# The last 64 features of FFN1, stacked into the seven block products

## The chip, the cores and the metric

The kernel runs on one core of a Trainium2 chip. The time is device microseconds from the start to the end of one execution, taken as the median of several runs; the kernel before takes 1108.99 us (three runs, 1108.16 to 1109.24).

A core has a matrix engine (TensorE, PE in the profile, with its weight loads as PEld), a vector engine (VectorE, DVE), an engine for activation functions (ScalarE, ACT), a general engine (GpSimd, POOL) and an engine that here only issues transfers (SyncE, SP). Each executes its instructions in order and waits on semaphores for the others. Transfers between the device's memory and the on-chip memory are put on a queue by SP, ACT or POOL and carried out by 16 DMA engines.

## The reference

A transformer block in which attention and the feed-forward part work on the same normalised input, and both are added to the input. S is 2048 rows, D is 576 features, F is 4608 hidden features; everything is float32.

```python
xn = layernorm(x)                      # over the 576 features, no weights
q, k, v = xn @ wqkv                    # 32 heads of 18 features
# row s attends to rows s, s-2, ..., s-14 (8 keys, window dilated by 2)
attn = softmax(q . k * 18**-0.5)       # over those 8 keys
a = (attn @ v) @ wo
h = xn @ w1 + b1                       # FFN1: 576 -> 4608
h = maximum(h, 0) ** 2                 # squared relu
out = x + a + (h @ w2 + b2)            # FFN2: 4608 -> 576
```

## The kernel before

**Precision.** A float32 number is split into a high part, as TensorE's float32r keeps it (a copy by ScalarE), and a low part, the rest (a subtraction by VectorE). A product is then three matmuls: high by high, low by high, high by low. "Split" below always means this pair of instructions, `..._hi` on ScalarE and `..._lo` on VectorE.

**Tiling.** The 2048 rows are four blocks of 512 (`TB`), b = 0 to 3. Matmuls are 128 by 128 weights against 512 rows. The 576 features are 512 in four chunks of 128, and 64 that are left over (`x4`). For those 64 the operand holds the features twice, once high and once low in the other 64 partitions, so that two matmuls (`left`) do the three products.

**Stages.** Query, key and value for the first blocks; FFN1 for blocks 0 and 1 together, stage s = 0 (`phase_a(0)`); FFN2 and output for block 1, with the queries, keys and values of blocks 2 and 3 (`phase_b0`); FFN1 for blocks 2 and 3, stage s = 1 (`phase_a(1)`); FFN2 and output for block 3 (`phase_b1`). During a `phase_a` the even block's FFN2 runs along, one pair behind.

**A pair.** `ffn_pair(s, p, work)` computes 2 x 128 hidden features for two blocks of rows, p = 0 to 17. The 512 features in two halves, the two hidden tiles and the two row blocks make a 2 by 2 block product, done with seven block products instead of eight: `B11`, `T1`, `T2`, `T3`, `B21`, `B22`, `T4`, where `T` stands for sums of weight blocks. Their other operands are X, and sums of the rows in `SS[1]`, `SS[2]`, `SS[3]`. Each product is six matmuls (two chunks, three split parts). They accumulate in three PSUM banks, `ba`, `bb`, `bc`:

- `B11` into `ba`, copied to `bb` by ScalarE; `T1` into `bc`;
- `T2` onto `bb`; ScalarE copies `bb` to `u[:, 0]`; then `T3` onto `bb`, copied to `u[:, 1]`;
- VectorE adds `bc` and `u[:, 1]`; `B21` onto `ba`; then `B22` onto `bc`, to which VectorE adds `u[:, 0]`; `T4` onto `bb`.

Then relu with bias, and squares, on ScalarE. The left 64 features add four calls of `left`, two matmuls each. Between the products stand four pieces of `work(i)`, seven matmuls each: FFN2 of the pair before. A pair is 42 + 8 + 28 = 78 matmuls.

**Order of the work.** It is written out by hand: in the five engine queues the instructions stand in the order in which the Python code issues them. A pair does besides: the square split of the pair before (`square_lo`), the next pair's FFN1 weights, which in stage 1 come back ready split from device memory (`w1_again`, 1024 KB twice, on ACT's queue), and two w2 splits (`w2_hi`, `w2_lo`, after which SP loads the w2 tile three ahead, `load_w2`).

**Attention** fills VectorE's time. `side(k)` issues k more steps of it. One unit (one row block, eight heads) has 18 steps: eight for query by key (a product and a sum for each of four row groups), one with the maximum and the subtraction, one that begins with the exponential on ScalarE, and eight for the weighted values. A call with `exp=False` stops ahead of the exponential. In stage 1 a pair has `side(3)` after `T1`, `side(2)` after `B22`, and `side(2, False)` at its end; pair 1 has `side(1)` for the first. Queries, keys and values of a unit come through three `kv` buffers, loaded on POOL's queue; `release()` tells that a buffer is free and issues the next load. Output rows of block 1's attention stand in one of the three until `o_hi(1, 4)`.

Other buffers that matter: `w1r` (two), free in stage 1 until the residual of block 2 is loaded into one ahead of pair 17; `mb`, `x40`, `x41`, `x4d` (one each), and `S1`, which holds `SS[1]`.

Of the kernel before, what the change touches and what calls it, by code (L numbers as in the profile page):

```python
# [8 lines left out]
F32 = mybir.dt.float32  # L9
# [7 lines left out]
P = 128  # L17
S, D, F = 2048, 576, 4608
H, DH, W, DIL = 32, 18, 8, 2
TB = 512  # L20
# [22 lines left out]


@with_exitstack
def block_kernel(ctx: ExitStack, tc: tile.TileContext, x, xt, wqkv, wo, w1, b1, w2, b2, out):
# [44 lines left out]
    oscr = {(b, k): dram.tile([P, NJ * G, z - a], F32, name=f"o{b}{k}") for b in range(NB) for k, (a, z) in enumerate(OPART)}  # L91
    mrscr = {b: dram.tile([2 * NJ, P], F32, name=f"mr{b}") for b in range(1, NB)}
    w1scr = [[dram.tile([P, 16 * P], F32, name=f"w1{p}{k}") for k in range(2)] for p in range(NP)]
    hscr = [[dram.tile([P, 2 * TB], F32, name=f"h{s}{p}") for p in range(NP)] for s in range(2)]

    def flat(t, off, parts, n):
# [6 lines left out]
    def tt(out, a, b, op):  # L103
        return nc.vector.tensor_tensor(out=out, in0=a, in1=b, op=op)  # L104
# [80 lines left out]
    def soon(f):  # L185
        if defer[0]:
            later.append(f)
        else:
            f()
# [5 lines left out]
    def normalize(b):  # L195
        open_x(b)
        for a in (0, 2):
            v = xm[b][:, a:a + 2]
            for k, op in enumerate((ALU.subtract, ALU.mult)):
                tt(v, v, mb[b][:, k:k + 1].to_broadcast([P, 2, TB]), op)  # L200
                if k:
                    soon(lambda v=v, a=a: nc.scalar.activation(X[b][:, 0, a:a + 2], v, AF.Copy))
                yield
        for k, op in enumerate((ALU.subtract, ALU.mult)):
            tt(xf[b], xf[b], mb[b][:, k], op)
        soon(lambda: left_hi(x4[b], xf[b]))
# [150 lines left out]
    def release():  # L357
        free[0] += 1
        fetch()
# [174 lines left out]
    def tile_products(b, n, h):  # L534
        hi, lo = products(h[:, 0, n % 2], h[:, 1, n % 2], w2s.pop((b, n)))
        return hi + lo

    hs, prev = {}, {}
    F_BANKS = [(5, 6, 7), (2, 3, 4)]

    def ffn_pair(s, p, work, first=False):
        b0, b1 = 2 * s, 2 * s + 1
        n = s * NP + p
        ba, bb, bc = (bank(i) for i in F_BANKS[s])
        f0, f1 = 2 * p, 2 * p + 1
        last = p == NP - 1
        A11 = lambda k, c: X[b0][:, k, c]
        A12 = lambda k, c: X[b0][:, k, 2 + c]
        A22 = lambda k, c: X[b1][:, k, 2 + c]
        S4 = lambda k, c: X[b1][:, k, c]  # L550
        ss = lambda i: lambda k, c: SS[i][:, k, c]

        def weight(slot, k, c):
            return w1s[n, slot // 4][:, k, slot % 4, c * P:(c + 1) * P]

        def product(to, slot, a, start=False):
            mm = [(weight(slot, 0, c), a(0, c)) for c in range(2)]
            for c in range(2):
                mm += [(weight(slot, 1, c), a(0, c)), (weight(slot, 0, c), a(1, c))]
            for i, (l, r) in enumerate(mm):  # L560
                nc.tensor.matmul(to, l, r, start=start and i == 0, stop=i == len(mm) - 1, skip_group_check=True)  # L561

        def left(to, f, v):
            for k in range(2):
                nc.tensor.matmul(to, weight(LEFT, k, f), v, start=False, stop=k == 1, skip_group_check=True)  # L565

        def relu(to, a, f):
            nc.scalar.activation(to, a, AF.Relu, bias=b1t[:, f:f + 1])  # L568

        def square_hi(r):  # L570
            h = mt.tile([P, 2, 2, TB], F32R, name="h", bufs=3)
            nc.scalar.activation(h[:, 0], r, AF.Square)
            return h

        def square(r):
            nc.scalar.activation(r, r, AF.Square)  # L576
# [12 lines left out]
        before = prev.pop("finish", None)  # L589
        product(ba, B11, A11, start=True)  # L590
        if first:
            nc.tensor.matmul(bb, weight(B11, 0, 0), A11(0, 0), start=True, stop=True, skip_group_check=True)
        nc.scalar.activation(bb, ba, AF.Copy)
        product(bc, T1, ss(1), start=True)
        if before:
            next(before, None)
        if not last:
            w1_again(n + 1, 0) if s else combine_w1(n + 1)
        if not first:
            side(1 if p == 1 else 3 if s else 2 + p % 2, s == 1)  # L600
# [6 lines left out]
        nc.scalar.activation(u[:, 0], bb, AF.Copy)  # L607
        if not first:
            left(bc, 1, x4[b1])
        work(1)  # L610
        if before:
            next(before, None)

        def splits():
            if not own_w2:
                w2_lo()
            if not last and not s:
                w1_hi(n + 1, 0)
            if not own_w2:
                w2_hi()  # L620
            if not last and not s:
                w1_lo(n + 1, 0)
            if not own_w2:
                w2_lo()

        if not first:
            splits()
        product(bb, T3, ss(3))
        if first:
            left(bc, 1, x4[b1])  # L630
        nc.scalar.activation(u[:, 1], bb, AF.Copy)
# [12 lines left out]
        relu(r0[:, 0], ba, f0)  # L644
        work(2)

        def third():
            product(bc, B22, S4)
            left(bc, 1, x4["d"])
            if not first:  # L650
                side(2)
            tt(r0[:, 1], bc, u[:, 0], ALU.add)
            relu(r0[:, 1], r0[:, 1], f1)

        def fourth():
            product(bb, T4, A22)
            left(bb, 0, x4[b1])
            relu(r1[:, 0], bb, f0)

        if first:  # L660
            fourth()
            third()
            work(2.5)
            h0 = square_hi(r0)
            square(r0)
        else:
            third()
            h0 = square_hi(r0)
            square(r0)
            fourth()  # L670
        side(2, False)
        hs[n] = h0
        prev["r"] = r0, r1, h0
        prev["finish"] = finish_pair()
        work(3)

    def phase_a(s, filler):
# [3 lines left out]
        for p in range(1, NP):  # L681
            h, ops = hs.pop(s * NP + p - 1), []

            def work(i):
                if i in (0, 2):
                    ops.extend(tile_products(b, 2 * p - 2 + i // 2, h))
                add(b, ops[7 * i:7 * i + 7])

            if p == NP - 1:
                complete(b)  # L690
                regroup(b, 0)
                regroup(b, 1)
                residual(b)
                if s == 0:
                    load_xt(2)
                    load_mb(2)
            ffn_pair(s, p, work)
        h, end = hs.pop(s * NP + NP - 1), prev.pop("finish")
        load_h(s, 0)
        next(end)  # L700
# [53 lines left out]
    def o_hi(b, c):  # L754
# [17 lines left out]
        nc.vector.transpose(t[:, 0].rearrange("p (u k f) -> p u k f", k=2, f=n),  # L772
                            ob[b, 1][:, :, None, OB - n:].to_broadcast([P, NJ * G, 2, n]))
        if b == 1:
            release()
        nc.scalar.activation(t[:, 1].bitcast(F32R), t[:, 0], AF.Copy)

    def o_lo(b, c):
# [16 lines left out]
    def residual(b):  # L795
        if b == 1:
            xr[b] = [mt.tile([P, NC - 1, TB], F32, name="h", bufs=3)]
        else:
            xr[b] = [sb.tile([P, NC - 1, TB], F32, name="w1r", bufs=2)]
        nc.sync.dma_start(xr[b][0], xt[b, :, :NC - 1])  # L800
# [179 lines left out]
    def phase_b0():  # L980
# [120 lines left out]
        def filler(i):  # L1101
            if i < 2:
                quads(1, 1, [len(steps) - 2 + i])
            if i == 1:
                for g in (2, 3):
                    offer(2, g)
                for g in range(G):
                    offer(3, g)
# [401 lines left out]
```

## Time and profile before

| | us |
|---|---|
| median of three runs | 1108.99 |
| the profiled execution | 1108.98 |
| its span, first to last instruction | 1107.3 |
| TensorE busy in the span | 1099.9 |
| VectorE busy | 871.6 |
| ScalarE busy | 558.7 |
| GpSimd busy | 115.8 |

The granted TensorE clock is 0.999 over the span. The mean of all transfers is 255 GB/s.

In the stage that is edited, from 652.5 to 951.5 us of the span (pairs 1 to 17 with s = 1), VectorE is busy for 219.0 of 299.0 us, ScalarE for 148.8.

How to read it: the page gives busy time by engine, the chain of work that ended last, and the costliest groups of instructions by line of the code. A row of a timeline has the start and the length in us, the engine, the line, the operation, the tiles written and read, and in square brackets how long the engine stood idle before and what ended that. `L104` is the helper for every VectorE operation on two tensors, so such rows are told apart by their tiles. Windows give the busy time of each engine in a stretch of the span. A DMA's "landing" is the time from its issue to its completion.

### The profile page before, as it was taken

The page shows a single profiled execution, that of the slowest core. Times are in us where ns is not written, and L with a number is a line of the kernel's source. Part 1 is how long each engine was busy: PE and PEld are TensorE (multiplying, and loading weights), DVE is VectorE, ACT ScalarE, POOL GpSimd, SP SyncE. Part 2 cuts the span into 40 slices and gives each one's busy share as a digit, 9 for nine tenths or more (in the row PEclk, how much of TensorE's full clock was granted, in tenths as well). Part 3 has the DMA queues.
Part 4 walks back from the last instruction along what each step waited for, and adds up shares of the span by engine and source line. Part 5 has one row for each costly group of instructions (what it writes and reads, how often), then busy time and mean ns, then how long its engine had stood idle before and what let it go on. Part 6 is the DMA issues. An engine that isn't in the chain of part 4 may idle for free.

```text
span 1107.3 us, 13777 instructions
## 1 busy us (share of the span) xinstructions
PE 1099.9 (99%) x4966; PEld 928.2 (84%) x4966; DVE 871.6 (79%) x1148; ACT 558.7 (50%) x787; POOL 115.8 (10%) x219
## 2 busy tenths in 40 slices
PE   9999999999999999999999999999999999999998
PEld 7998888888888888888899888888888888888887
DVE  7686979897996979999979477686767778699655
ACT  5435765556566654455344345454554545533342
POOL 4000101020020100100010200210202102010100
PEclk9999999999999999999999999999999999999999
DMA  8956987889799686866755976858668596665862
GB/s 297 333 179 237 336 297 257 301 199 361 261 246 379 232 351 213 310 232 227 255 169 160 324 267 238 318 187 308 230 244 292 194 332 241 229 219 199 279 189 85
DMA packets 97332, 282.56 MB, mean 255 GB/s; under 512 B 12904, under 2 KB 41328, under 8 KB 82544
## 3 DMA queue, kind: packets, MB, share of 16 engines
q1 hardware_dynamic: 62336, 182.90, 47.7%
q0 software_dynamic: 10544, 52.14, 13.2%
q10 hardware_dynamic: 24384, 46.64, 12.9%
q8 instruction: 39, 0.64, 0.2%
q14 instruction: 29, 0.24, 0.1%
HBM read 200.16 MB, written 81.48 MB: 254 GB/s over the span
## 4 chain that ended last, share of the span: by engine, by line
PE 95%; DVE 2%; DMA 1%; issue 1%; ACT 0%; POOL 0%; ACTq 0%; DVEq 0%; POOLq 0%
PE p L530 45%; PE p L561 30%; PE p L332 7%; PE p L565 6%; PE p L937 6%; PE p L941 1%; PE p L1294 1%; DMA w1s<-w 1%; DVE pr L104 0%; DVE w2s L104 0%; PE p L1211 0%; DVE h L104 0%; DVE w1s L104 0%; PE p L1256 0%; DVE r L104 0%
## 5 line engine op out<-in xcount | busy, mean ns | idle before, releaser
L530 PE MATMUL p<-h,w2s 128*128 128x512 f32 x2066 | 491.7, 389 | 0.3 <-DVE w2s L104 0.2
L530 PEld LDWEIGHTS p<-h,w2s 128*128 128x128 f32 x2066 | 387.6, 188 | 81.9 <-DVE w2s L104 0.6
L561 PE MATMUL p<-X,w1s 128*128 128x512 f32 x864 | 219.3, 389 | 0.0
L561 PEld LDWEIGHTS p<-X,w1s 128*128 128x128 f32 x864 | 162.2, 188 | 33.6
L503 ACT ACTIVATE w2s<-w2r 128x640 fp32r<-128x640 f32 x164 | 120.1, 735 | 138.2 <-PE p L530 112.8
L104 DVE TENSOR_TENSOR w2s<-w2r,w2s 128x576 fp32r<-128x576 f32 x164 | 123.4, 754 | 70.8 <-ACT w2s L503 70.6
L561 PE MATMUL p<-S,w1s 128*128 128x512 f32 x648 | 164.7, 389 | 0.5 <-ACT r L607 0.5
L561 PEld LDWEIGHTS p<-S,w1s 128*128 128x128 f32 x648 | 121.5, 188 | 26.1 <-ACT r L607 0.9
L409 POOL DMA_DIRECT2D o<-q x128 | 69.4, 607 | 593.5 <-DVE q L104 591.6
L568 ACT ACTIVATE r<-r,b1t 128x512 f32<-128x512 f32 x72 | 52.0, 722 | 130.5 <-DVE r L104 130.5
L381 DVE TENSOR_REDUCE lg<-pr 128x64 f32<-128x1152 f32 x64 | 86.5, 1352 | 1.5
L104 DVE TENSOR_TENSOR pr<-lg,kv 128x1152 f32<-128x1152 f32 x64 | 86.7, 1355 | 1.2
L104 DVE TENSOR_TENSOR pr<-q,kv 128x1152 f32<-128x1152 f32 x64 | 86.6, 1353 | 0.8
L104 DVE TENSOR_TENSOR r<-p,r 128x512 f32<-128x512 f32 (+1 forms) x77 | 53.0, 689 | 35.3 <-PE p L565 22.7
L104 DVE TENSOR_TENSOR pr<-pr 128x576 f32<-128x576 f32 (+1 forms) x128 | 77.6, 606 | 3.2
L576 ACT ACTIVATE r<-r 128x1024 f32<-128x1024 f32 x72 | 76.2, 1058 | 1.2
L104 DVE TENSOR_TENSOR h<-r,h 128x1024 fp32r<-128x1024 f32 (+3 forms) x46 | 51.8, 1137 | 29.4 <-ACT r L576 20.7
L565 PE MATMUL p<-x,w1s 128*128 128x512 f32 x216 | 66.6, 390 | 0.2 <-DMA w1s<-w 0.2
L104 DVE TENSOR_TENSOR w1s<-w1r,w1s 128x1024 fp32r<-128x1024 f32 (+1 forms) x42 | 50.3, 1199 | 16.7 <-ACT w1s L471 13.7
L607 ACT ACTIVATE r<-p 128x512 f32<-128x512 f32 x36 | 21.6, 600 | 68.1 <-PE p L561 67.7
L568 ACT ACTIVATE r<-p,b1t 128x512 f32<-128x512 f32 x72 | 48.4, 673 | 0.9 <-DMA out<-r 0.5
L565 PEld LDWEIGHTS p<-x,w1s 128*128 128x128 f32 x216 | 40.5, 188 | 9.0 <-DMA w1s<-w 0.6
(172 smaller groups left out, 1092.7 us busy)
## 6 DMA issues: line engine op xcount, KB each, us to landing
w2r<-in_w SPq DMA_DIRECT2D x144, 320.0 KB, 3.6
kv<-kvq POOLq DMA_DIRECT2D x29, 1296.0 KB, 8.4
w<-w1s SPq DMA_DIRECT2D x36, 1024.0 KB, 8.5
w1s<-w ACTq DMA_DIRECT2D x34, 1024.0 KB, 5.9
h<-r SPq DMA_DIRECT2D x36, 512.0 KB, 6.4
h<-h SPq DMA_DIRECT2D x36, 512.0 KB, 3.9
w1r<-in_w SPq DMA_DIRECT2D x18, 640.0 KB, 7.5
kvq<-st ACTq DMA_DIRECT2D x48, 216.0 KB, 3.2
```

The source lines that it names most:

```text
L104: return nc.vector.tensor_tensor(out=out, in0=a, in1=b, op=op)
L332: nc.tensor.matmul(p[:, :QW], l, r, start=k == 0, stop=k == len(mm) - 1)
L381: nc.vector.tensor_reduce(out=lg[:, j * HG:(j + 1) * HG].rearrange("p a w -> p w a"), in_=pr.rearrange("p w (a d) -> p w a d", d=DH), axis ...
L409: nc.gpsimd.dma_start(rows[:, i], q[i * L:(i + 1) * L, :, a:z])
L503: nc.scalar.activation(w2s[stream[i]][:, :DE], raw2[i], AF.Copy)
L530: nc.tensor.matmul(yp[b][c], v, a, start=c not in yb[b], stop=c in last and c not in [o[0] for o in ops[i + 1:]], skip_group_check=True)
L561: nc.tensor.matmul(to, l, r, start=start and i == 0, stop=i == len(mm) - 1, skip_group_check=True)
L565: nc.tensor.matmul(to, weight(LEFT, k, f), v, start=False, stop=k == 1, skip_group_check=True)
L568: nc.scalar.activation(to, a, AF.Relu, bias=b1t[:, f:f + 1])
L576: nc.scalar.activation(r, r, AF.Square)
L607: nc.scalar.activation(u[:, 0], bb, AF.Copy)
L937: nc.tensor.matmul(to, l[:, js], r, start=start and n == 0, stop=n == len(mm) - 1, skip_group_check=True)
```

## The change

In pairs 2 to 17 of stage 1 the left 64 features are treated as two halves of 32, as the 512 are as two halves of 256, and so take part in the same seven block products. For each of the seven there is a stack of 128 partitions: the 32 features' high part, their low part, their high part again, and 32 partitions of zeros; the weights stand against it as high, high, low, low. One matmul does the three split products. So `left` returns at once in these pairs, and each product gets a seventh matmul, at its end:

```diff
+            if stacked:
+                mm.append((LW[p % 2][:, STACK[slot]], ST[slot]))
...
         def left(to, f, v):
+            if stacked:
+                return
```

A pair then has 49 + 28 = 77 matmuls.

*The row stacks.* After the normalisation of blocks 2 and 3, SP stores their 64 left features in device memory (`xlscr`). In pair 0, a memset clears the last 32 partitions of a `w1r` tile, and six loads on SP bring the 32-feature halves back three times over (`load_left_rows`). In pair 1 VectorE makes the four sums (`stack_sums`) in the `kv` buffer that block 1's attention output leaves at `o_hi(1, 4)`; it is released only in pair 2, after the last stack is made. Splits turn rows and sums into the seven stacks: four in the other `w1r` buffer (pair 1), one in `x40` (pair 1), two in `x41` and `x4d` (pair 2).

```diff
+        if ready:
+            left_weight_sums()
+        if s and p == 2:
+            one_stack(T3, "x41")
+            one_stack(B22, "x4d")
+            one_stack_lo(T3)
+            one_stack_lo(B22)
+            release()
+        if s and p == 1:
+            stack_sums()
+            open_stacks()
+            stack_hi(LR["st"][:, 0:2], LR["a"][:, 0:2])
+            stack_hi(ST[T4], LR["a"][:, 3])
         if not first:
             side(1 if p == 1 else 3 if s else 2 + p % 2, s == 1)
...
+            if ready:
+                left_weight_hi(p + 1)
+            if s and p == 1:
+                stack_lo(LR["st"][:, 0:2], LR["a"][:, 0:2])
+                stack_lo(ST[T4], LR["a"][:, 3])
+                stack_hi(ST[T1], LR["s"][:, 0])
             if not own_w2:
                 w2_hi()
...
+            if ready:
+                left_weight_lo(p + 1)
             if not own_w2:
                 w2_lo()
...
+        if s and p == 1:
+            open_left_weights()
+            load_left_weights(2)
+            stack_lo(ST[T1], LR["s"][:, 0])
+            one_stack(T2, "x40")
         work(2)
...
             product(bc, B22, S4)
             left(bc, 1, x4["d"])
-            if not first:
+            if s and p == 1:
+                one_stack_lo(T2)
+                left_weight_sums()
+                left_weight_hi(2)
+            elif not first:
                 side(2)
...
+        if s and p == 1:
+            left_weight_lo(2)
         side(2, False)
```

*The weight stacks.* A new input `w1l` holds the left weights of each pair, repeated to 128 partitions (256 KB a pair). For the pair that follows, SP loads them into the `mb` buffer, VectorE makes the sums, ScalarE and VectorE split them into one of two halves of a `w1r` buffer; the load for the pair after goes out behind the split:

```diff
+    def left_weight_sums():
+        r = LR["w"]
+        tt(r[:, 0:2], r[:, 3:5], r[:, 2:4], ALU.subtract)
+        tt(r[:, 3], r[:, 4], r[:, 0], ALU.subtract)
+        tt(r[:, 6], r[:, 5], r[:, 3], ALU.subtract)
+
+    def left_weight_hi(p):
+        nc.scalar.activation(LW[p % 2], LR["w"], AF.Copy)
+
+    def left_weight_lo(p):
+        rows = slice(2 * L, P)
+        tt(LW[p % 2][rows], LR["w"][rows], LW[p % 2][rows].bitcast(F32), ALU.subtract)
+        load_left_weights(p + 1)
```

In pairs 2 to 16 these are the three parts marked `ready`; for pair 2 they are done in pair 1.

*What moves.* Pair 1 has no `side(2)` after `B22`. The `release()` at `o_hi(1, 4)` moves to pair 2. The residual of block 2 is loaded after pair 17 into `S1`, no longer ahead of pair 17 into a `w1r` buffer.

More of the change, by code (lines that the diff above doesn't have):

```diff
@@ L45, in block_kernel @@
 @with_exitstack
-def block_kernel(ctx: ExitStack, tc: tile.TileContext, x, xt, wqkv, wo, w1, b1, w2, b2, out):
+def block_kernel(ctx: ExitStack, tc: tile.TileContext, x, xt, wqkv, wo, w1, b1, w2, b2, w1l, out):
     nc = tc.nc
@@ L93, in block_kernel @@
     w1scr = [[dram.tile([P, 16 * P], F32, name=f"w1{p}{k}") for k in range(2)] for p in range(NP)]
+    xlscr = {b: dram.tile([2 * L, TB], F32, name=f"xl{b}") for b in (2, 3)}
     hscr = [[dram.tile([P, 2 * TB], F32, name=f"h{s}{p}") for p in range(NP)] for s in range(2)]
@@ L205, in normalize @@
             tt(xf[b], xf[b], mb[b][:, k], op)
+        if b in xlscr:
+            nc.sync.dma_start(xlscr[b], xf[b][:2 * L])
         soon(lambda: left_hi(x4[b], xf[b]))
@@ L536, in tile_products, with load_left_rows, stack_sums, stack_hi @@
         return hi + lo
+    ST, LW, LR = {}, {}, {}
+    STACK = {T1: 0, T3: 1, B11: 2, T2: 3, B22: 4, B21: 5, T4: 6}
+    def load_left_rows():
+        t = LR["a"] = sb.tile([P, 4, TB], F32, name="w1r", bufs=2)
+        nc.vector.memset(t[3 * L:], 0.0)
+        for g in range(3):
+            for k, b in enumerate((2, 3)):
+                nc.sync.dma_start(t[g * L:(g + 1) * L, 2 * k:2 * k + 2], xlscr[b].rearrange("(q r) t -> r q t", q=2))
+    def stack_sums():
+        a, z = LR["a"], LR["s"]
+        tt(z[:, 0], a[:, 2], a[:, 3], ALU.add)
+        tt(z[:, 2], a[:, 0], a[:, 2], ALU.subtract)
+        tt(z[:, 1], z[:, 0], a[:, 0], ALU.subtract)
+        tt(z[:, 3], a[:, 1], z[:, 1], ALU.subtract)
+    def stack_hi(to, v):
+        nc.scalar.activation(to, v, AF.Copy)
+    def stack_lo(to, v):
+        rows = slice(L, 2 * L)
+        tt(to[rows], v[rows], to[rows].bitcast(F32), ALU.subtract)
+    def open_stacks():
+        t = LR["st"] = sb.tile([P, 4, TB], F32R, name="w1r", bufs=2)
+        for i, k in enumerate((B11, B21, T4, T1)):
+            ST[k] = t[:, i]
+    def one_stack(k, name):
+        ST[k] = mt.tile([P, TB], F32R, name=name)
+        stack_hi(ST[k], LR["s"][:, {T2: 1, T3: 2, B22: 3}[k]])
+    def one_stack_lo(k):
+        stack_lo(ST[k], LR["s"][:, {T2: 1, T3: 2, B22: 3}[k]])
+    def open_left_weights():
+        t = sb.tile([P, 2, 7, P], F32R, name="w1r", bufs=2)
+        LR["w"] = sb.tile([P, 7, P], F32, name="mb")
+        LW[0], LW[1] = t[:, 0], t[:, 1]
+    def load_left_weights(p):
+        if p < NP:
+            nc.sync.dma_start(LR["w"][:, 2:6], w1l[p])
+    def left_weight_sums():
[9 more added lines that the diff above has]
+        load_left_weights(p + 1)
     hs, prev = {}, {}
@@ L546, in ffn_pair @@
         last = p == NP - 1
+        stacked = s == 1 and p > 1
+        ready = s == 1 and p > 1 and not last
         A11 = lambda k, c: X[b0][:, k, c]
@@ L692, in phase_a @@
                 regroup(b, 1)
-                residual(b)
                 if s == 0:
+                    residual(b)
                     load_xt(2)
@@ L697, in phase_a @@
             ffn_pair(s, p, work)
+        if s:
+            residual(b)
         h, end = hs.pop(s * NP + NP - 1), prev.pop("finish")
@@ L774, in o_hi @@
         if b == 1:
-            release()
+            LR["s"] = sb.tile([P, 4, TB], F32, name="kv", bufs=3)
         nc.scalar.activation(t[:, 1].bitcast(F32R), t[:, 0], AF.Copy)
@@ L797, in residual @@
             xr[b] = [mt.tile([P, NC - 1, TB], F32, name="h", bufs=3)]
+        elif b == 2:
+            xr[b] = [mt.tile([P, NC - 1, TB], F32, name="S1")]
         else:
@@ L1104, in filler @@
             if i == 1:
+                load_left_rows()
                 for g in (2, 3):
@@ L1487 @@
     w1 = np.concatenate(w1, 2).reshape(NP, P, 5, 2 * P)
+    w1l = np.asarray(B_w1)[DM:].reshape(2, L, NP, 2, P)
+    w1l = np.stack([w1l[q, :, :, f] for q, f in ((0, 0), (0, 1), (1, 1), (1, 0))], 2)
+    w1l = np.tile(w1l.transpose(1, 0, 2, 3), (1, G, 1, 1))
     x = np.asarray(A_x).reshape(S, D)
@@ L1498 @@
         "b2": rows(np.asarray(B_b2).reshape(D, 1)).reshape(NC, P).T,
+        "w1l": w1l,
     }
```

## The prediction

> **What bounds the kernel now.** I read the first and fourth parts of the page, then the busy time by stage, then the chain of waits inside the stage that is edited.
>
> ```profile
> span 1107.3 us, 13777 instructions
> PE 1099.9 (99%) x4966; PEld 928.2 (84%) x4966; DVE 871.6 (79%) x1148; ACT 558.7 (50%) x787; POOL 115.8 (10%) x219
> PE 95%; DVE 2%; DMA 1%; issue 1%; ACT 0%; POOL 0%; ACTq 0%; DVEq 0%; POOLq 0%
> ```
>
> TensorE is busy for 99% of the span and makes 95% of the chain that ends last: a matmul less is time less, as long as nothing makes TensorE wait. The stages (columns: stretch, length, busy time of PE, PEld, DVE, ACT, POOL, granted clock, DMA share, GB/s):
>
> ```profile
> 652.50:951.50 299.00, 299.00 (x1321) 247.56 (x1320) 218.98 (x271) 148.83 (x207) 37.54 (x69) 1.00 0.74 264
> 652.50:670.20 17.70, 17.70 (x80) 14.64 (x79) 11.89 (x17) 7.15 (x10) 0.54 (x1) 1.00 0.95 349
> 670.20:687.90 17.70, 17.70 (x80) 14.66 (x79) 13.49 (x20) 9.17 (x14) 0.00 (x0) 1.00 0.59 211
> ```
>
> The first row is pairs 1 to 17 of the second FFN1 stage, the next two are pair 1 and pair 2. TensorE has no idle time there, the clock is 1.00, and VectorE is busy for 219 of 299 us. The chain over pair 2 (start, length, what):
>
> ```profile
> 670.21 2.72 PE p L561 x12
> 672.93 1.59 PE p L530 x7
> ...
> 686.30 1.59 PE p L530 x7
> ```
>
> It is TensorE alone. By the code a pair holds 78 matmuls (42 in products, 8 left, 28 of FFN2), and from 670.21 to 686.30 + 1.59 = 687.89 they take 17.68 us: 0.2267 us for one.
>
> **The gain.** Pairs 2 to 17 lose 8 left matmuls each and get 7 stacked ones of the same 128x512 shape: 16 x 0.2267 = **3.63 us**. The stacked weights fill all 128 rows, the left ones did too; nothing in the trace prices rows. [...]
>
> **Steady pairs (3 to 17).** Every pair up to 16 gets, for the next pair, on VectorE three weight sums (128x256, 128x128, 128x128) and one low part (64x896), on ScalarE one high part (128x896), on SP one 256 KB load. Prices (line, columns: total, mean ns):
>
> ```profile
> L104 DVE TENSOR_TENSOR w2s<-w2r,w2s 128x576 fp32r<-128x576 f32 x36 | 27.1, 754 | 31.6 <-ACT w2s L503 31.6
> L104 DVE TENSOR_TENSOR h<-r,h 128x1024 fp32r<-128x1024 f32 x16 | 19.6, 1226 | 7.8 <-ACT r L576 7.1
> L104 DVE TENSOR_TENSOR q<-pr 128x144 f32<-128x144 f32 x24 | 7.4, 308 | 0.8
> L104 DVE TENSOR_TENSOR lg<-lg,mx 128x256 f32<-128x256 f32 x7 | 3.0, 425 | 0.2
> L104 DVE TENSOR_TENSOR h<-p,h 128x512 f32<-128x512 f32 x4 | 2.5, 684 | 0.0
> L381 DVE TENSOR_REDUCE lg<-pr 128x64 f32<-128x1152 f32 x26 | 35.1, 1351 | 0.5
> ```
> ```profile
> L576 ACT ACTIVATE r<-r 128x1024 f32<-128x1024 f32 x32 | 33.8, 1058 | 0.5
> L503 ACT ACTIVATE w2s<-w2r 128x640 fp32r<-128x640 f32 x34 | 25.0, 734 | 24.5 <-PE p L530 24.5
> ```
>
> Sums: 0.43 + 0.31 + 0.31 = 1.05 us; the low part lies between 0.75 (576) and 1.23 (1024), by length 1.09; the high part between 0.73 and 1.06, 0.95. Pair 7 has the softmax's exponential at its start, the worst place, so I lay them in there:
>
> ```profile
> 758.45 1.52 PE L561 MATMUL p<-X,w1s 128*128 128x512 f32 x6
> ...
> 758.91 1.23 DVE L104 TENSOR_TENSOR h<-r,h 128x1024 fp32r<-128x1024 f32 x1 [0.33 <-ACT r L576]
> ...
> 764.31 0.60 ACT L607 ACTIVATE r<-p 128x512 f32<-128x512 f32 x1 [1.77 <-PE p L561]
> ...
> 766.35 0.74 ACT L503 ACTIVATE w2s<-w2r 128x640 fp32r<-128x640 f32 x1 [1.44 <-PE p L530]
> ...
> 767.13 0.76 DVE L104 TENSOR_TENSOR w2s<-w2r,w2s 128x576 fp32r<-128x576 f32 x1 [1.85 <-ACT w2s L503]
> ...
> 768.35 0.69 DVE L104 TENSOR_TENSOR r<-p,r 128x512 f32<-128x512 f32 x1 [0.46 <-ACT r L631]
> ...
> 770.91 1.52 PE L561 MATMUL p<-X,w1s 128*128 128x512 f32 x6
> ```
>
> The sums delay the exponential, and by it the copy of the T2 product (764.31), by 1.05; that copy idles 1.77 now. The high part goes into the 1.44 before the second w2 split. VectorE takes 1.05 + 1.09 = 2.14 into the idle 1.85 + 0.46 = 2.31. The addition at 768.35 must be over when B22 (770.91) overwrites its bank; it is 1.9 us early, which covers what is left over. So I cost these at nothing. Without that cover each of 15 pairs would pay up to 2.1 us. The load is issued after the low part, which follows the copy and the high part: 764.31 + 0.60 + 0.95 + 1.09 = 767.0 at the earliest and with T2 ending later some 767.7, 9.2 us into the pair. It is read behind the square split, 758.91 + 1.23 - 758.45 = 1.7 us into the next. A pair being 77 x 0.2267 = 17.46, the load has 9.9 us. The slowest w2 load of pairs 2 to 17 is in pair 9:
>
> ```profile
> DMA to landing us min/median/max: 9.8/10.3/10.7
> ```
>
> So a late one costs VectorE 0 to 0.8 us, inside the 1.9 us; I take 0.
>
> **The way in: pairs 1 and 2.** Here the stacks are built, and the cover is thin. Pair 1 gets on VectorE four 128x512 sums, low parts of 1024, 512, 512 and 512 columns, the weight sums and the low part; it loses the two side steps of its third slot. What stands there now:
>
> ```profile
> 656.24 0.74 DVE L104 TENSOR_TENSOR w2s<-w2r,w2s 128x576 fp32r<-128x576 f32 x1
> 656.91 1.34 DVE L381 TENSOR_REDUCE lg<-pr 128x64 f32<-128x1152 f32 x1
> ...
> 661.05 0.76 DVE L104 TENSOR_TENSOR w2s<-w2r,w2s 128x576 fp32r<-128x576 f32 x1 [2.13 <-ACT w2s L503]
> ...
> 670.05 1.52 PE L561 MATMUL p<-X,w1s 128*128 128x512 f32 x6
> ...
> 673.11 0.40 ACT L390 ACTIVATE lg<-lg 128x256 f32<-128x256 f32 x1
> 673.41 0.73 ACT L503 ACTIVATE w2s<-w2r 128x640 fp32r<-128x640 f32 x1
> ```
>
> Consecutive VectorE rows overlap by 0.07 (656.24 + 0.74 against 656.91), which I take off each. Until the second w2 low part is done: 656.24 + 0.74 + 4 x 0.68 + 1.34 + 0.75 + 1.23 + 0.68 + 0.75 - 7 x 0.07 = 664.0. SP issues the w2 load behind it, then the first stacked-weight load, at about **664.3**. Call its landing L. From L, in the order of the code: sums 1.05, high part 0.95, low part 1.09: the weights are ready at L + 3.1. TensorE wants them at pair 2's seventh matmul, 670.05 + 6 x 0.2267 = **671.4**. Behind the waiting sums on VectorE stands the addition that frees B22's bank for pair 2's T1 (due one matmul after 671.4): at L + 1.05 + 0.69 it is earlier than the weights, and adds nothing. VectorE goes on: two side steps 2.70, pair 1's square split 1.23, sums 1.05, two stack low parts 1.37, then the softmax maximum and subtraction (0.84; the lost steps move them here: before, pair 1 did them and pair 2 began with the exponential), then on ScalarE exponential 0.40, w2 split 0.73, copy of T2 0.60. Sum 8.9, less 8 x 0.07, and so L + **11.5**. T3 overwrites that bank 35 matmuls into pair 2, at 670.05 + 7.93 = **678.0**; each product being one longer gives no more than that. Any L over 666.5 stalls TensorE, us for us.
>
> How soon does the load land? The nearest rows are the 320 KB w2 loads on the same queue (minimum, median, maximum), over the stage, in pair 1 and in quiet pair 5:
>
> ```profile
> DMA to landing us min/median/max: 2.8/6.1/11.6
> ```
> ```profile
> DMA to landing us min/median/max: 2.8/9.7/11.6
> ```
> ```profile
> DMA to landing us min/median/max: 2.8/2.8/2.8
> ```
>
> Pair 1 is the crowded one (DMA share 0.95), but one of its transfers goes away, this attention load on POOL:
>
> ```profile
> 664.52 0.54 POOL L354 DMA_DIRECT2D kv<-kvq  x1 [16.79 <-DVE pr L104]
> ```
>
> POOL's k load for the next head group now waits for a side step after L, and its v load for the buffer that the stack sums keep until pair 2; both are read a pair later, and only the outputs of that attention queue behind them. So I take the stage's median, 6.1: L = 664.3 + 6.1 = 670.4. Then the stacked weights are 673.5 - 671.4 = 2.1 us late, and T3's bank 670.4 + 11.5 - 678.0 = **3.9 us** late, the first included in the second. The second weight load is issued at L + 3.1 and wanted at L + 6.8; I cost it at nothing because the SP queue is then empty, with 2.8 us as in the quiet pair. Bounds of this part: 0 (L below 666.5) to 664.3 + 11.6 + 11.5 - 678.0 = 9.4 us.
>
> **The rest.** In pair 0 a memset of 2048 columns is at most two of the 128x1024 rows, 2.45 us:
>
> ```profile
> 632.34 0.69 DVE L104 TENSOR_TENSOR r<-p,r 128x512 f32<-128x512 f32 x1 [1.69 <-PE p L565]
> 632.95 1.29 DVE L767 STREAM_TRANSPOSE r<-kv 128x512 f32<-128x512 f32 x2
> 635.37 1.29 DVE L104 TENSOR_TENSOR h<-r,h 128x512 fp32r<-128x512 f32 x2 [1.12 <-ACT h L768]
> ```
>
> It takes 1.69 idle us and pushes the next rows by 0.8, inside the 1.12 idle ahead of 635.37. The six row loads on SP and the two row stores of the stage before are read tens of us later; they hold SP behind a VectorE result that the following w2 load waits past anyway. The residual moves behind pair 17, ahead of an h load on SP; both are read only after FFN2's last two tiles and part of the o chunks. All at nothing; if the cover were gone, a 1024 KB transfer ahead of the h load.
>
> **Sum.** Profiled time 1108.98 (the median of the runs is 1108.99): 1108.98 - 3.63 + 3.9 = **1109.3 us**. The gain of sixteen pairs is paid back on the way into the second of them.
>
> **Rivals.**
> - *The first load lands as in a quiet queue* (2.8 us; for it: its rival on POOL is gone; against it: w1s and two w2 loads are still moving). L = 667.1, no wait for weights, T3 0.6 late: 1108.98 - 3.63 + 0.6 = **1106.0**. Faster by 0.2% needs L under 667.9, a landing under 3.6 us. [...]
> - *The first load lands as pair 1's w2 loads do* (9.7 to 11.6). T3 7.5 to 9.4 late: **1112.9 to 1114.8**. This is the other side; it decides from a landing of 8.0 us on, where the stall is 5.8.
> - *The second load is the late one*: 6.1 us instead of 3.7 makes VectorE wait 2.4 more ahead of the exponential: **1111.7**. For it: pair 2's w1s load starts close behind it.
>
> **How the numbers follow.** About 0.2% (2.2 us) is what a measurement of this kernel can tell. Forecast, within 0.2%: 0.48. Quiet load: 0.22, faster. Slower: crowded first load 0.15, late second load 0.15, together 0.30. The likeliest has 1106.8 to 1111.2 for its own; the range goes down to the quiet case less 0.2 and up to the low end of the crowded one, 1105.8 to 1112.9.
>
> **What would show it.** Right: 77 matmuls in 17.46 us in pairs 3 to 17 without idle TensorE; in pair 2 a wait of TensorE for VectorE at the first stacked matmul and one for ScalarE's T2 copy, together 3.9 us; the weight sums of pair 1 waiting for the load. Wrong: no wait in pair 2 (a quiet load, or steps in another order), waits at B22 in many pairs, or a stall at the stage's ends.

## The result and the profile after

The changed kernel takes 1115.24 us, median of six runs (1113.80 to 1115.48), against 1108.93 for the kernel before: a ratio of 1.0054, 95% interval 1.0041 to 1.0067. It is slower, and above the predicted range. The profiled execution has 6.5 us more span. The first part of the page:

```profile
span 1113.8 us, 13890 instructions
PE 1102.4 (99%) x4950; PEld 926.3 (83%) x4950; DVE 912.0 (82%) x1223; ACT 575.5 (52%) x809; POOL 115.2 (10%) x219
```

TensorE has 16 matmuls fewer (4950 for 4966), as foretold, and is busy for 2.5 us longer. Busy time by pair (columns as in the prediction; each stretch goes from the first matmul of a pair to the first of the next; these are pairs 2, 3 and 4):

```profile
670.60:693.57 22.97, 19.74 (x79) 15.45 (x77) 20.17 (x32) 13.28 (x19) 1.07 (x2) 0.93 0.72 277
693.57:711.26 17.69, 17.69 (x78) 14.48 (x77) 16.48 (x21) 10.36 (x15) 4.34 (x8) 1.00 0.66 223
711.26:728.95 17.69, 17.69 (x78) 14.48 (x77) 12.46 (x16) 9.67 (x14) 1.65 (x3) 1.00 0.87 340
```

Two things are seen. Pair 2 takes 22.97 us, at a granted clock of 0.93. And pairs 3 and 4, with TensorE busy throughout and no wait, take 17.69 us where 77 x 0.2267 = 17.46 was predicted; with 78 matmuls it was 17.68. The whole gain of a steady pair is missing, and the profile shows no idle time in its place.

Pair 2 on TensorE (start, length, what, and in brackets the idle time before it with what ended it):

```profile
670.60 1.52 PE L627 MATMUL p<-X,w1s 128*128 128x512 f32 x6
675.07 0.79 PE L627 MATMUL p<-w1r 128*128 128x512 f32 x1 [2.95 <-DVE w1r L105]
675.66 2.76 PE L627 MATMUL p<-S,w1s 128*128 128x512 f32 x6
678.22 0.47 PE L627 MATMUL p<-w1r 128*128 128x512 f32 x1
678.53 1.76 PE L533 MATMUL p<-h,w2s 128*128 128x512 f32 x7
...
683.76 1.66 PE L627 MATMUL p<-S,w1s 128*128 128x512 f32 x6 [0.28 <-ACT r L688]
```

The first stacked matmul (line 627, `p<-w1r`) waits 2.95 us for VectorE's part of the stacked weights. The six matmuls behind it take 678.22 - 675.66 = 2.56 us, 0.427 each: TensorE runs at about half speed for some 3 us, at a granted clock of 0.50 (third number from the right):

```profile
675.07:678.22 3.15, 3.15 (x7) 2.48 (x8) 3.12 (x3) 3.09 (x5) 0.54 (x1) 0.50 0.44 133
```

T3 (683.76) then waits 0.28 for ScalarE's copy of T2. The chain of waits ahead of T3 (start, length, what):

```profile
664.89 6.87 DMA mb<-in_w1l
...
671.78 0.44 DVE mb L105
...
672.95 0.95 ACT w1r L593
...
679.95 0.68 DVE x L105
680.63 0.60 DVE x4d L105
...
681.26 0.43 DVE mx L390
...
681.72 0.44 DVE lg L105
...
682.50 0.72 ACT w2s L506
683.22 0.49 ACT r L688
```

It is the predicted chain: first load, sums, high part, stack parts, softmax maximum and subtraction, w2 split, copy of T2. In the rows left out, from 673.89 to 679.88, this view follows ScalarE (relus, squares, the stacks' high parts) where the prediction followed VectorE; VectorE had no idle time there either, its weight sums ending at 679.92.

The account, from the first to the last matmul: -3.63 for 16 matmuls; +16 x (17.69 - 17.45) = +3.8 for slow pairs (17.45 is measured below); pair 2 22.97 - 17.69 = +5.3; and pair 2 begins at 670.60 instead of 670.05, +0.55, of which some 0.4 is there already when pair 1 starts. Together +6.0, of 6.5 in the span; the other 0.5 lie behind pair 17, and their cause was not looked for.

### The profile page after: what moved, and what is told of

Same layout as the page of the kernel before. It is cut to its first block, busy times and chain, and to the rows that moved or that the text cites. A ratio compares the mean times of both kernels' runs of the same rounds, so it can differ in the third digit from the quotient of the medians.

```text
span 1113.8 us, 13890 instructions
## 1 busy us (share of the span) xinstructions
PE 1102.4 (99%) x4950; PEld 926.3 (83%) x4950; DVE 912.0 (82%) x1223; ACT 575.5 (52%) x809; POOL 115.2 (10%) x219
## 4 chain that ended last, share of the span: by engine, by line
PE 92%; DVE 3%; DMA 2%; ACT 1%; issue 1%; POOL 0%; ACTq 0%; SPq 0%; DVEq 0%; POOLq 0%
PE p L533 46%; PE p L627 31%; PE p L1041 6%; PE p L335 5%; PE p L633 3%; PE p L1045 1%; DMA w1s<-w 1%; DMA mb<-in_w1l 1%; PE p L1399 1%; DVE h L105 0%; DVE w1r L105 0%; DVE pr L105 0%; DVE w1s L105 0%; DVE w2s L105 0%; DMA kv<-in_x 0%
## 5 line engine op out<-in xcount | busy, mean ns | idle before, releaser
L105 DVE TENSOR_TENSOR h<-h 128x1024 fp32r<-128x1024 f32 x36 | 43.9, 1221 | 5.4 <-ACT h L938 5.4
L533 PE MATMUL p<-w1s,w2s 128*128 128x512 f32 x195 | 44.7, 389 | 0.0
```

Source lines behind the costliest of these rows:

```text
L533: nc.tensor.matmul(yp[b][c], v, a, start=c not in yb[b], stop=c in last and c not in [o[0] for o in ops[i + 1:]], skip_group_check=True)
```

## The experiments

Two questions: why a steady pair gains nothing, and whether the chain from the first load is what pair 2 pays for. Times of runs with one execution have no interval.

### Is it the operands, or the work beside them?

Run e1, in `product`:

```
-                mm.append((LW[p % 2][:, STACK[slot]], ST[slot]))
+                mm.append((weight(slot, 0, 0), a(0, 0)))
```

> Leaves out: the stacked matmul of each product reads the product's own first weights and its own first 512 activation columns, not the stacked ones, so the last 64 features are missing from pairs 2 to 17 of the second stage. The preparation of the stacks and of the stacked weights stays. Theory A (the place of the operands: what a matmul reads from the tiles w1r, which lie behind the tiles of the other operands in SBUF, makes it and its neighbours take 230 to 236 ns instead of 226.7): the period of the steady pairs falls from 17.69 to 77 x 0.2267 = 17.46 us. Theory B (the added work of VectorE, ScalarE and the DMA beside the pair slows the matmuls): the period stays at 17.69 us. Both: the first stacked matmul of pair 2 waits for no weights.

Measured: 1111.91 us, and pair 3:

```profile
693.36:710.81 17.45, 17.45 (x78) 14.45 (x77) 15.84 (x21) 9.67 (x14) 4.34 (x8) 1.00 0.68 221
```

17.45 us with all of the preparation in place. So the added instructions and the load cost a steady pair nothing, as predicted, and theory B falls. What the stacked matmul reads makes the pair slow. Pair 2 did not get better for it (23.54 us, 669.82 to 693.36), although it waits for no stacked weights:

```profile
678.66 1.30 PE L533 MATMUL p<-h,w2s 128*128 128x512 f32 x5
682.27 3.30 PE L627 MATMUL p<-S,w1s 128*128 128x512 f32 x7 [2.31 <-ACT r L688]
```

The idle time has moved to T3, behind the same chain, and seven matmuls after it take 3.30 us: half speed again.

### Where the operands lie

The compiled kernels give each tile's address in a partition (these are no numbers of the profile). The tags lie one behind the other; `kv`, three tiles of 10368 bytes, stands ahead of `w1r`.

| tile | begins at byte | modulo 256 |
|---|---|---|
| `h`, `X0`, `x40`, `w1s`, `S1` to `S3`, `X1`, `x41`, `x4d`, `w2s` | 4832 to 127200 | 224 |
| `w1r` (stacks, stacked weights) | 163168, 171360 | 96 |
| `r4` (in the third stage, some of the QKV weights) | 196960 to 209248 | 96 |
| `xf` (one o chunk) | 220832 | 160 |

So `w1r` is different in two ways: it lies in the upper part of the on-chip memory (SBUF), and at another offset modulo 256. That 256 is the distance that counts is an assumption at this point; e5, e6 and e11 test it. Run e2 puts the operands of FFN1 up, all but part of `X0`, and FFN2's weights, with the offset kept (`h`, FFN2's rows, stays below 128 KB); run e3 shifts all of them by 128 bytes together. Both on the kernel before:

```
 e2
-    mt = ctx.enter_context(tc.tile_pool(name="mt", bufs=1))
+    const.tile([P, 8], F32, name="pad")
     sb = ctx.enter_context(tc.tile_pool(name="sb", bufs=1))
+    mt = ctx.enter_context(tc.tile_pool(name="mt", bufs=1))
 e3
     const = ctx.enter_context(tc.tile_pool(name="const", bufs=1))
+    const.tile([P, 32], F32, name="pad")
```

> The kernel before with the two big pools of SBUF in the other order: all operands of the FFN1 matmuls but part of one tile lie above 128 KB in each partition, at the same offset modulo 256 bytes as before; nothing else changes. Theory A (place, read as the upper part of SBUF): matmuls of 128x512 take about 233 ns instead of 226.7 wherever they read the upper part; a steady pair goes from 17.68 to as much as 78 x 0.2333 = 18.2 us, and the time to some 1109 + 33 x 0.5 = 1125 us. Rival A2 (place, read as the offset modulo 256 bytes) and theory B (the neighbours' work): 17.68 us and 1109 us, within 2.

> The kernel before with 128 bytes of padding ahead of both big pools: the operands stay in the lower part of SBUF, but at the offset modulo 256 bytes that the tiles w1r had. Rival A2 (offset modulo 256 bytes decides): a steady pair goes from 17.68 to as much as 18.2 us, the time to about 1125 us. Theory A (upper part) and theory B: 17.68 us and 1109 us, within 2.

Measured: 1108.87 and 1108.19 us, and a pair in each (e2, then e3):

```profile
705.28:722.96 17.68, 17.68 (x79) 14.64 (x78) 12.54 (x17) 9.14 (x14) 0.54 (x1) 1.00 0.79 292
```
```profile
704.59:722.27 17.68, 17.68 (x79) 14.64 (x78) 12.54 (x17) 9.14 (x14) 0.54 (x1) 1.00 0.79 292
```

Neither the upper part nor the offset by itself costs anything, a pair taking the 17.68 us of the kernel before in both: my theory A and its rival A2 both fell. What was left is that in both runs all operands of these pairs still shared one offset. Theory A3: matmuls are slow where the operands' offsets *differ*. Its rival was the content of the stacks. Run e5 gives `w1r` the offset 224 in the changed kernel (the tags behind it in the pool move by the same 128 bytes; none of them is an operand of these pairs); run e6 takes the common offset away from the FFN2 weights in the kernel before, and e11 does it with 32 bytes:

```
 e5, ahead of the first w1r tile
+    sb.tile([P, 32], F32, name="pad")
 e6, in w2_hi (e11: [P, 8])
+        if i == 0:
+            mt.tile([P, 32], F32, name="pad")
```

> The changed kernel with 128 bytes of padding between two tags of SBUF, so that the tiles w1r (stacks and stacked weights) get the same offset modulo 256 bytes as all other matmul operands; nothing else changes. Theory A3 (a matmul is slow where its two operands, or those of neighbouring matmuls, differ in this offset): 77 matmuls take 17.46 us in the steady pairs, and the time falls by some 3.6 from 1115.2 to 1111.6 us; the waits in pair 2 stay. Rival E (it is what the stacks hold, three groups of 32 rows and a fourth of zeros, not where they lie): 17.69 us and 1115 us, within 1.

> The kernel before with 128 bytes of padding ahead of the FFN2 weights (tag w2s) alone, so that they differ from the activations in their offset modulo 256 bytes. Theory A3: the 28 FFN2 matmuls of a pair, and some behind them, take 230 to 236 ns instead of 226.7; a pair takes 17.85 us or more instead of 17.68, and the time is 6 to 12 us over 1108.7 us. Rival E (what the operands hold): 17.68 us and 1108.7 us, within 1.

> As the run e6, with 32 bytes of padding instead of 128: the FFN2 weights differ from the activations by 32 bytes in their offset. If any difference within 256 bytes counts alike: a pair of 17.84 us and some 1122 us, as in e6. If only a difference of 64 bytes or more counts: 17.68 us and 1108.7 us.

Measured: e5 1111.49 us (1.0028 of before, 1.0018 to 1.0038), 3.75 less than the changed kernel; e6 1121.97 us, 13 over the kernel before; e11 1127.42 us. Pairs of e5 (pairs 3 and 4), of e6 and of e11:

```profile
693.02:710.47 17.45, 17.45 (x78) 14.46 (x77) 16.52 (x22) 10.44 (x15) 4.33 (x8) 1.00 0.66 231
710.47:727.92 17.45, 17.45 (x78) 14.46 (x77) 12.51 (x16) 9.67 (x14) 1.65 (x3) 1.00 0.89 344
```
```profile
712.38:730.22 17.84, 17.84 (x80) 14.67 (x78) 12.55 (x17) 9.13 (x14) 0.54 (x1) 1.00 0.77 276
```
```profile
715.35:733.32 17.97, 17.97 (x79) 14.64 (x78) 12.53 (x17) 9.12 (x14) 0.54 (x1) 1.00 0.76 281
```

A pad of 128 bytes gives the changed kernel its 17.45, and the same pad in another place costs 0.16 us a pair in a kernel that had no fault. In e5 `w1r` begins at 163296, which is 619 x 256 bytes behind `h`: so a difference of a multiple of 256 costs nothing (17.45 us) where one of 128 does (17.69). Run e6 costs 13 us where 6 to 12 were expected, and e11 takes neither of its two expected values. The groups of the steady pairs show what to look for (line, columns: total, mean ns of one); first the changed kernel, then e5:

```profile
L533 PE MATMUL p<-h,w2s 128*128 128x512 f32 x341 | 86.5, 392 | 0.0
L627 PE MATMUL p<-w1r 128*128 128x512 f32 x48 | 18.9, 394 | 0.0
L627 PE MATMUL p<-x,w1r 128*128 128x512 f32 x24 | 9.5, 397 | 0.0
```
```profile
L534 PE MATMUL p<-h,w2s 128*128 128x512 f32 x349 | 87.1, 389 | 0.0
L628 PE MATMUL p<-w1r 128*128 128x512 f32 x49 | 19.1, 389 | 0.0
L628 PE MATMUL p<-x,w1r 128*128 128x512 f32 x24 | 9.3, 389 | 0.0
```

In e5, where the offsets agree, the mean is 389 ns in all three. In the changed kernel it is 397 and 394 for the stacked matmuls, and 392 for FFN2 matmuls, which are the same as before: a stacked matmul slows some of its neighbours too.

Run e7 takes the two operands apart, one choice for each pair:

```
+                lw, st, w, v = LW[p % 2][:, STACK[slot]], ST[slot], weight(slot, 0, 0), a(0, 0)
+                mm.append({4: (lw, v), 5: (w, st), 6: (w, ST[T2]), 7: (w, ST[B11]), 8: (lw, ST[T2]), 9: (w, v),
...
```

> The changed kernel with other operands for the seven stacked matmuls in pairs 4 to 12, one choice for each pair (weights / activations): 4 stacked / product's own; 5 own / stack; 6 own / one stack in the low tile x40; 7 own / one stack in w1r; 8 stacked / the stack in x40; 9 own / own; 10 own / the stacked weights read as activations; 11 128 columns of the stack in x40 / own; 12 the same of a stack in w1r / own; from 13 on the first 96 rows of both. The results of these pairs are wrong: the last 64 features are missing from 4 to 12. Theory A3 (offset modulo 256 bytes): pairs 6, 9 and 11 take 17.46 us, the others more, up to 17.7 where both or the activations lie in w1r. Rival E (what they hold): 9 and perhaps 4 take 17.46, 6, 8 and 11 are slow too, and from 13 on (no zero rows) the pair is 17.46.

Pairs 4 to 13, in this order (the second number is the pair's length):

```profile
710.81:728.37 17.56, 17.56 (x78) 14.48 (x77) 12.47 (x16) 9.65 (x14) 1.65 (x3) 1.00 0.85 334
728.37:745.85 17.48, 17.48 (x78) 14.45 (x77) 15.01 (x23) 9.94 (x15) 0.00 (x0) 1.00 0.65 241
745.85:763.30 17.45, 17.45 (x78) 14.45 (x77) 15.66 (x20) 9.70 (x14) 5.03 (x10) 1.00 0.65 221
763.30:780.80 17.50, 17.50 (x78) 14.45 (x77) 14.56 (x21) 9.99 (x15) 0.92 (x2) 1.00 0.97 366
780.80:798.35 17.55, 17.55 (x78) 14.48 (x77) 15.76 (x24) 9.70 (x14) 0.50 (x1) 1.00 0.59 207
798.35:815.80 17.45, 17.45 (x78) 14.45 (x77) 15.48 (x17) 9.66 (x14) 5.47 (x11) 1.00 0.82 285
815.80:833.30 17.50, 17.50 (x78) 14.45 (x77) 14.71 (x24) 10.11 (x15) 0.00 (x0) 1.00 0.84 308
833.30:850.76 17.46, 17.46 (x79) 14.45 (x77) 15.83 (x21) 9.68 (x14) 4.31 (x8) 1.00 0.65 221
850.76:868.30 17.54, 17.54 (x78) 14.48 (x77) 12.51 (x16) 9.69 (x14) 1.65 (x3) 1.00 0.86 332
868.30:886.01 17.71, 17.71 (x78) 14.50 (x77) 15.10 (x23) 10.03 (x15) 0.00 (x0) 1.00 0.67 238
```

Pairs 6, 9 and 11 are the fast ones, 17.45 to 17.46. Pairs 6 and 11 read a stack, the one in `x40`, as activations and as weights: what a stack holds doesn't matter. Activations in `w1r` (7 and 10) cost 0.05 / 7 = 7 ns a matmul (in pair 5 only four of the seven lie there); weights there (4, 8, 12) 0.09 to 0.11 / 7 = 13 to 16; both, 0.24 / 7 = 34. With 96 rows and no zero rows (13) the pair is slow all the same. Rival E falls.

One thing in these numbers goes beyond theory A3. In four of the seven products of the changed kernel both operands of the stacked matmul lie in `w1r`, so their offsets are equal, and yet these matmuls have a mean of 394 ns and the pair is the slowest kind. What differs there is the offset against the matmuls before and behind. In pair 2 of the changed kernel the weights of T2's stacked matmul load from 681.26 to 681.45, while the last of the six matmuls ahead, which end at 681.66, still runs. So the rows of one matmul may meet the weights of the next; no run takes this apart.

### Pair 2

Run e4 issues the first load at the start of pair 1:

```
         if s and p == 1:
+            LR["w"] = sb.tile([P, 7, P], F32, name="mb")
+            load_left_weights(2)
             stack_sums()
...
             open_left_weights()
-            load_left_weights(2)
```

> The first load of stacked weights is issued at the start of pair 1 instead of before its third part; its sums stay where they are. Theory C (the chain from this load through the sums is what makes pair 2 stall: 2.95 us for the weights, then matmuls at half speed, then 0.3 for the bank of T3): the wait and the half speed vanish, and the time falls by about 6 us from 1115.2 to 1109.2 us, not below, since the steady pairs still gain nothing. Rival D (VectorE and ScalarE have too many steps there, whenever the load comes): a wait of 2 us or more for the weights or for the copy of T2 stays, and the time stays above 1111.5 us.

Measured: 1112.25 us, median of eight (1110.23 to 1114.10), 1.0032 of before (1.0022 to 1.0043). In the profiled run (1111.46) TensorE's waits around pair 2 are:

```profile
PE p L626 <- ACT r L689: 1.0, 1, 1.0
```

The wait for the weights and the half speed are gone; 1.0 us for T3's bank is left, and pair 2 takes 19.0 us (670.78 to 689.79) instead of 22.97. Theory C holds for the profiled run. The median fell by 3 and not by 6 us, to a value over the 1111.5 that rival D asks for, and the runs spread over 4 us. By the code the load now follows output stores and the store of `h` on SP, so that its landing may differ from run to run; this is not shown. Run e8 keeps this place, with the pad of e5, and with

```
-            side(1 if p == 1 else 3 if s else 2 + p % 2, s == 1)
+            side(1 if p == 1 else 2 if s and p == 2 else 3 if s else 2 + p % 2, s == 1)
```

> The changed kernel with the padding of the run e5, the early load of the run e4, and two side steps instead of three at the start of pair 2, so that the softmax exponential no longer stands ahead of the copy of T2. Theories A3 and C together: steady pairs of 17.46 us, no wait of TensorE in pair 2; 1108.7 - 3.6 = 1105.1 us, up to 1107 with what is left at the start. If A3 falls: 1108.7 us or more. If C falls: a wait of over 1 us in pair 2, and 1107 us or more.

Measured: 1108.65 us, median of twelve, from 1107.06 to 1113.03; 1.0001 of before (0.9990 to 1.0012). In its profiled run (1110.13) the weight sums wait for the load again, though it was issued some 6 us sooner than in the changed kernel, and T3's bank is late by 1.8 us, what was expected if theory C fell:

```profile
DVE mb L106 <- DMA mb<-in_w1l: 1.9, 1, 1.9
```
```profile
682.17 1.66 PE L627 MATMUL p<-S,w1s 128*128 128x512 f32 x6 [1.82 <-ACT r L690]
683.67 0.39 PE L627 MATMUL p<-x,w1r 128*128 128x512 f32 x1
```

Two lessons: issuing into a crowded queue is not issuing early (the load took 11.0 us to land, in the changed kernel 6.9); and my edit of the side steps did nothing for T3, since the second step begins with the exponential and so still stands ahead of the copy (680.59 and 681.54 on ScalarE). Run e9 therefore issues the load behind the row loads, before the stage, with three side steps and the pad of e5; e10 leaves out all three; e12 makes them up in pairs 3 to 7:

```
 e9, at the end of load_left_rows
+        LR["w"] = sb.tile([P, 7, P], F32, name="mb")
+        load_left_weights(2)
 e10, as e9, and
+            side(1 if p == 1 else 0 if s and p == 2 else 3 if s else 2 + p % 2, s == 1)
 e12, as e10, and at the end of ffn_pair
-        side(2, False)
+        side(3 if s and 2 < p < 8 else 2, False)
```

> The changed kernel with the padding of the run e5, three side steps at the start of pair 2 as in the changed kernel, and the first load of stacked weights issued right behind the six row loads, before the second FFN1 stage, where no two 512 KB stores share the queue with it. Theory C in its narrow form (the load's landing is the late link): the weight sums wait for nothing, pair 2 waits 0 for the weights and 1.0 us for T3's bank, as in the run e4; the time is 1108.7 - 3.6 + 1.0 + 0.3 = 1106.4 us, and it spreads no more than the kernel before (2 us). Rival D (too many steps on VectorE and ScalarE): a wait of 2 us or more, 1107.5 us or more.

> The run e9 with none of the three side steps at the start of pair 2, so that softmax maximum, subtraction and exponential come after the copy of T2. The chain of the prediction (side steps, stack parts, maximum, subtraction, exponential, copy of T2) says that T3's wait of 1.0 us goes with them: 1108.7 - 3.6 + 0.3 = 1105.4 us. If the copy of T2 is late for another reason, a wait of 0.5 us or more for T3's bank stays and the time is that of e9; if the steps are missed later, a wait shows up in pair 3 or at the end of the stage.

> The run e10 with a third side step instead of two at the end of each of pairs 3 to 7, which makes up the steps that pairs 1 and 2 left out. If the wait of 1.5 us for VectorE at the end of the stage in e10 came from these missed steps, it goes, no pair gets a wait for it, and with the offset, the early load and the copy of T2 the time is 1108.7 - 3.6 + 0.4 = 1105.5 us, up to 1106.5. If the steps hold up the pairs that they are moved to, or the end waits for something else, it stays at that of e10, 1108.4 us.

Measured against the kernel before: e9 1107.50 us (0.9991, 0.9982 to 1.0000), e10 1108.37 us (0.9994, 0.9985 to 1.0003), e12 1106.17 us (0.9976, 0.9967 to 0.9985; eleven runs, 1105.13 to 1107.14). All waits of TensorE from 655 to 1000 us, e9 and then e10:

```profile
PE p L629 <- ACT r L690: 1.1, 1, 1.1
```
```profile
PE p L534 <- DVE S L919: 1.5, 1, 1.5
```

In e9 the weights are no longer late (their load takes 5.7 us to land), and T3's 1.1 us is what remains, the size that e4 had. (Its runs, from 1106.39 to 1111.13, spread more than the 2 us expected; ten of the eleven lie within 2.4.) In e10 that wait is gone, so the steps ahead of the copy were its cause; but the missed steps have to be done before the stage can end, and TensorE waits 1.5 us there. In e12 this view lists nothing, and pairs 2 and 3 take what 77 matmuls take:

```profile
670.26:687.72 17.46, 17.46 (x79) 14.46 (x77) 14.63 (x22) 12.44 (x18) 1.07 (x2) 1.00 0.88 332
687.72:705.17 17.45, 17.45 (x78) 14.46 (x77) 15.80 (x24) 9.67 (x14) 0.49 (x1) 1.00 0.67 242
```

Its profiled run's span is 1104.2 us, 3.1 under that of the kernel before, of the 3.63 that the removed matmuls are worth.

## Why the prediction was wrong, point by point

- **The gain (3.63 us).** The count was right. The step that failed is "7 stacked ones of the same 128x512 shape: 16 x 0.2267": the pairs took 17.69 us, not 17.46, and 16 x 0.24 = 3.8 us came back. I wrote that "nothing in the trace prices rows" and looked no further for what else differs in the stacked operands. The trace of before did hold a warning, an operand of another offset (`xf`):

```profile
L530 PE MATMUL p<-xf,w2s 128*128 128x512 f32 x9 | 2.3, 394 | 0.0
L530 PE MATMUL p<-h,w2s 128*128 128x512 f32 x5 | 1.3, 389 | 0.0
```

  Same shape, weights of the same tag, and 394 ns against 389. But the same trace also has operands of another offset that cost nothing: in the third stage, where 432 columns stream, those from `r4` (`r`, offset 96) against `x40` and `x41` (`x`, 224) take 357 ns, as do those from `w1s` against sums, both at 224:

```profile
L941 PE MATMUL p<-r,x 128*128 128x432 f32 x48 | 12.0, 357 | 0.0
L937 PE MATMUL p<-w1s,S 128*128 128x432 f32 x144 | 30.1, 357 | 0.0
```

- **Steady pairs cost nothing.** Right: e1 and e5 have all their added work and take 17.45 us.
- **The way in, 3.9 us.** The mechanism was right and the sizes were off. T3 starts at 683.76; without a stall it would have been 670.60 + 35 x 0.2267 = 678.53, so it is 5.2 late. The load was issued at 664.89 (predicted 664.3) and took 6.87 (6.1), which makes the landing 1.4 late; from there to the end of the copy, 683.71, it is 11.9 us (11.5); the pair itself begins 0.55 later. 3.9 + 1.4 + 0.4 - 0.55 = 5.2. "The first included in the second" held: e1 takes away the wait for the weights, and T3's wait grows to 2.31.
- **Half speed.** Not foreseen: the stall of the weights was taken to cost its length alone. Here it cost little beyond, since T3 still waits 0.28 us for the chain after it.
- **The second load at nothing.** Right: VectorE waits for one load only in pair 2.
- **The rest at nothing.** Pair 2 begins 0.55 us later. 0.39 of it is there at the start of pair 1, where the runs e9, e10 and e12 have +0.35, +1.40 and +0.03 with the same row loads, so it is within what runs differ by.
- **The rivals.** The time, 1115.24, lies above the forecast's range and also above that of the crowded first load (1112.9 to 1114.8). It is slower, as that rival would have it, but not by it: the landing was 6.87 us, under the 8.0 from which that rival decides, and more than half of the miss is the missing gain, which no rival held. The quiet load did not come, nor the late second one.

What stays open: why a difference of 128 bytes costs nothing in the 128x432 matmuls of the third stage; why a difference of 32 bytes costs a pair more (0.29 us, e11) than one of 128 (0.16, e6); why the neighbours of a stacked matmul are slow for a while; and the spread of e4, e8 and e9, whose longest executions were not profiled.

## What to carry to other kernels

Give all operands of a stream of 128x512 matmuls like this one the same offset modulo 256 bytes (17.45 us a pair in e5 against 17.69); for other shapes, measure. A tag whose buffers together are no multiple of 256 bytes, such as the three of 10368 here, shifts all that lie behind it (`w1r` to 96, where 224 is the others' offset), and nothing in the profile names the cause: look for a group of matmuls whose mean is some ns over that of others of its shape (394 and 397 against 389 here). When an edit adds a chain of work ahead of a busy engine, move its first transfer to where it lands soon (in e9, ahead of the stage, 5.7 us after its issue; in e8 11.0), and place moved steps by the copy that the engine waits for (1.1 us in e9); steps left out must be made up before the stage's end (1.5 us in e10).

## What the hardware showed that I had not expected

- A 128x512 matmul's pace depends on how the addresses of its operands, and of its neighbours', stand to each other: a pair of 78 takes 17.68 us with equal offsets modulo 256, 17.84 with its 28 FFN2 weights 128 bytes off, 17.97 with 32 bytes. In e7 and the changed kernel the place of the weights and of the activations, one or both, costs 7 to 34 ns a stacked matmul.
- After an idle time of 2.95 us the changed kernel's TensorE ran at a granted clock of 0.50 for 3.15 us, which leaves 0.93 for pair 2. After 2.31 us (e1) seven matmuls took 685.41 - 682.27 = 3.14 us, 0.449 each; in e5, with 2.5 us, the clock of pair 2 (670.67 to 693.02) was 0.92. After 1.82 us (e8) there was no half speed: the six matmuls behind that wait took 683.67 - 682.17 = 1.50 us. The length of the idle time alone does not decide it: in e7 TensorE waited 2.6 us for the same weights, and the clock behind it was 1.00:

```profile
674.61:677.76 3.15, 3.15 (x14) 2.58 (x15) 3.12 (x3) 3.09 (x5) 0.54 (x1) 1.00 0.51 123
```

  In 3.15 us it started 14 matmuls there, in the changed kernel 7. What else decides stays open.
